# Two chunks of weights by plain products, and new durations for the order

## The chip, the cores and the metric

The kernel runs on one core of one Trainium2 chip. The metric is the time of one execution on the device in microseconds (us).

## The reference

Three parts follow each other. First comes linear attention with 4 batches, 8 heads, 576 tokens and a head size of 64; each head's output is normalised. Its 2304 tokens by 512 columns are x. Then x is multiplied by w_a and w_b (512 x 1536), the two results are multiplied element by element, and that by w_out (1536 x 512). Last comes a layer with a softmax in the middle.

```python
kv = einsum('bhsd,bhse->bhde', k, v)
o = einsum('bhsd,bhde->bhse', q, kv)
x = o / sqrt(mean(o * o, -1) + 1e-06) * g_norm     # to 2304 x 512
y = (x @ w_a) * (x @ w_b) @ w_out
h = y @ w_in                                       # 512 x 1024
s = h * softmax(h)
out = (s - mean(s)) / sqrt(var(s) + 1e-06) * g_ln @ w_out2
```

The weights arrive as 64-bit floats and are decoded on the chip.

## The kernel before

Each matrix product is made of float32 operands that are split in two: a high part (a copy rounded to the type that TensorE multiplies, `hi_of`) and a low part (what is left, `lo_of`). A product is then three matmuls, high by high, high by low and low by high (`three`, L668 to L671).

The work has three stages on TensorE.

1. Attention. Each of 20 tiles of at most 128 tokens goes through `att_1` (L557): a product with the matrix kv, a square and a copy on ScalarE, a sum on VectorE (L589), a power on GpSimd (L592) and a scaling on VectorE (L593). `att_2` (L598) transposes the tile on TensorE and writes it to x, scaled by g_norm (L620). Beside it the units of the products with w_a and w_b begin.
2. Those units (`Unit`, L682). x is cut into three thirds of 768 tokens, and each third into four quarters: A11, A12 are the upper and lower half of the 512 columns for the first 384 tokens; the other two belong to the second 384. The 1536 columns of w_a and w_b are cut into twelve chunks f of 128. For a chunk and a third, seven products of quarters (P1 to P7, `PROD`) take the place of eight. They need sums of quarters of x (S1 to S4, `x_blocks`, L630) and sums of quarters of the weights (T1 to T4, `w_sums`, L385). Each product has two halves of columns by three matmuls, so a unit has 42 matmuls of 384 columns. The results g go to DRAM.
3. The product with w_out (L1094): g and w_out come back from DRAM by `fetch` (L832), are split (L837, L838) and multiplied in six blocks of 384 tokens, y. Meanwhile w_in and w_out2 are decoded. Then the last layer runs (L1206, L1291, and L669 to L671 again).

Every chunk of weights is loaded in raw form by SyncE's queue (`load_one`, L262) and decoded by one ScalarE and five VectorE instructions and an addition (`decode`, L309 to L356).

The order of instructions on each engine is fixed when the kernel is built. The class `Order` (L46) keeps a clock for ScalarE ("A"), VectorE ("V") and GpSimd ("G"); each operation has a reckoned duration there. Where a tuple such as "GV" with two durations is given, the engine that would end sooner takes it, VectorE's duration counted twice (`PRICE`). Of operations that are due, the one of lowest rank goes first. TensorE's work is chosen by the main loop: `next_unit` (L846) has at most two units in work, of the first two chunks that are not through, and steps of attention go in between on a credit. DMAs of all kinds are issued by SyncE's queue, in the order in which the loop comes to them, and a DMA that waits holds those behind it.

In `x_blocks` the operations of third t have rank 1.2 + t and 1.1 + t; the tiles of attention have rank 1 + third. A tile of the last third waits in `back_ready` (L513) until its place in x4 is free.

## Time and profile before

| | before |
|---|---|
| median of 3 runs | 773.57 us (771.54 to 774.11) |
| profiled execution | 772.95 us, its span 771.0 us |
| TensorE busy | 699.9 us, 91% of the span |
| VectorE busy | 525.7 us, 68% |
| ScalarE busy | 313.0 us, 41% |
| GpSimd busy | 305.2 us, 40% |
| mean granted clock of TensorE | 0.96 |

The span goes from the first to the last instruction of the profiled execution; the time of that execution includes what lies around it. PE is TensorE, PEld its loads of weights, DVE VectorE, ACT ScalarE, POOL GpSimd, SPq the queue of SyncE. A clock of 1.00 is 2.4 GHz.

### The profile page before, as it was taken

Reading aid. Unit: us, or ns where it says so; the run is one execution under the profiler, and the core shown is the slowest. Engines: PE = TensorE matmul, PEld = TensorE weight load, DVE = VectorE, ACT = ScalarE, POOL = GpSimd, SP = SyncE. Lnnn points to the kernel's source line nnn. Section 1 sums busy time; section 2 is a strip of 40 time slices with the busy share of each in tenths; the row PEclk is TensorE's granted clock in tenths of the full one; section 3 lists DMA queues with packets and bytes.
Section 4 is the critical chain, followed back from the end, with each engine's and each line's share of the span. In section 5 each row is a group of like instructions: output and inputs, shape, how many; then the busy total and the mean of one; then the engine's idle time right before and its main releaser. Section 6 shows DMA issues by size and latency. Waiting matters only on the chain. (4 is left out here: it accounts for less than half of the span.)

```text
span 771.0 us, 10606 instructions
## 1 busy us (share of the span) xinstructions
PE 699.9 (91%) x3916; PEld 640.5 (83%) x3916; DVE 525.7 (68%) x792; ACT 313.0 (41%) x603; POOL 305.2 (40%) x272
## 2 busy tenths in 40 slices
PE   5768867889999998899989979998999999999998
PEld 4658756789998998889889979988987888888887
DVE  3768776687677777885366889786239494587661
ACT  3654734433333333322364444344144444344331
POOL 0655673344153334441372676423035353344110
PEclk9767978999999999999999989999999999999999
DMA  9725301044343433442286534675600000000001
GB/s 305 296 86 192 119 28 42 21 151 144 110 158 130 137 110 132 141 148 99 89 280 212 180 99 137 216 246 159 237 2 15 28 15 28 18 25 27 28 28 42
DMA packets 37652, 89.83 MB, mean 117 GB/s; under 512 B 4448, under 2 KB 14944, under 8 KB 37600
## 3 DMA queue, kind: packets, MB, share of 16 engines
q1 hardware_dynamic: 37600, 89.15, 33.6%
q8 instruction: 31, 0.51, 0.3%
q14 instruction: 21, 0.17, 0.1%
HBM read 62.92 MB, written 26.21 MB: 116 GB/s over the span
## 5 line engine op out<-in xcount | busy, mean ns | idle before, releaser
L1094 PE MATMUL ps<-regl,regh 128*128 128x384 f32 x384 | 74.4, 351 | 10.0 <-ACT y L1098 8.1
L1094 PEld LDWEIGHTS ps<-regl,regh 128*128 128x128 f32 x384 | 70.6, 199 | 12.5 <-ACT y L1098 9.7
L356 POOL TENSOR_TENSOR wf_w<-wf_w,u_w 128x512 f32<-128x512 f32 x20 | 27.2, 1360 | 80.8 <-DVE u_w L345 80.8
L669 PE MATMUL ps<-xh,wCh 128*128 128x384 f32 x144 | 51.2, 356 | 7.9 <-ACT xh L154 4.6
L592 POOL TENSOR_TENSOR r<-r,mhalf 128x8 f32<-128x8 f32 (+1 forms) x20 | 37.9, 1908 | 50.3 <-ACT r L591 41.5
L754 DVE TENSOR_TENSOR g<-ps,s 128x384 f32<-128x384 f32 x36 | 20.0, 556 | 54.1 <-PE ps L671 38.1
L669 PE MATMUL ps<-xh,wAh 128*128 128x384 f32 x144 | 50.6, 352 | 4.6 <-ACT xh L154 1.5
L838 DVE TENSOR_TENSOR regl<-regl 128x384 fp32r<-128x384 f32 x51 | 42.8, 856 | 17.0 <-ACT regl L837 16.7
L670 PE MATMUL ps<-xl,wBh 128*128 128x384 f32 x144 | 48.9, 340 | 5.9 <-DVE xl L640 5.9
L670 PE MATMUL ps<-xl,wCh 128*128 128x384 f32 x144 | 50.2, 349 | 4.3 <-DVE xl L640 4.3
L669 PE MATMUL ps<-xh,wBh 128*128 128x384 f32 x144 | 50.3, 349 | 3.4 <-ACT xh L154 1.3
L670 PE MATMUL ps<-xl,wAh 128*128 128x384 f32 x144 | 50.1, 348 | 1.2 <-POOL xl L640 1.2
L671 PE MATMUL ps<-xh,wCl 128*128 128x384 f32 x144 | 49.9, 346 | 0.5 <-POOL wCl L413 0.5
L671 PE MATMUL ps<-xh,wAl 128*128 128x384 f32 x144 | 50.2, 348 | 0.1
L671 PE MATMUL ps<-xh,wBl 128*128 128x384 f32 x144 | 48.6, 337 | 0.0
L736 ACT COPY ps<-ps 128x384 f32<-128x384 f32 x36 | 16.7, 464 | 76.4 <-PE ps L671 51.1
L837 ACT CAST regl<-regl 128x384 fp32r<-128x384 f32 (+1 forms) x56 | 28.9, 523 | 36.0 <-DMA regl<-gd 35.8
L1301 DVE TENSOR_TENSOR dl<-t,regl 128x1024 fp32r<-128x1024 f32 x18 | 21.8, 1218 | 30.6 <-ACT regl L1300 30.5
L1094 PE MATMUL ps<-regl,regl 128*128 128x384 f32 x228 | 40.5, 334 | 0.0
L1094 PEld LDWEIGHTS ps<-regl,regl 128*128 128x128 f32 x228 | 39.6, 188 | 0.0
L1206 PE MATMUL h<-bo,aop 128*128 128x512 f32 x150 | 38.2, 395 | 0.0
L669 PE MATMUL out<-regh,regl 128*128 128x512 f32 (+1 forms) x95 | 36.8, 387 | 1.1 <-DVE dl L1301 1.1
(172 smaller groups left out, 1966.7 us busy)
## 6 DMA issues: line engine op xcount, KB each, us to landing
raw_w<-in_w SPq DMA_DIRECT2D x36, 512.0 KB, 3.5
gd<-g SPq DMA_DIRECT2D x36, 384.0 KB, 2.3
regl<-gd SPq DMA_DIRECT2D x51, 192.0 KB, 3.1
kv<-in_kv SPq DMA_DIRECT2D x16, 512.0 KB, 6.6
out<-us SPq DMA_DIRECT2D x17, 256.0 KB, 2.0
raw_i<-in_w_in SPq DMA_DIRECT2D x8, 512.0 KB, 3.6
raw_o<-in_w_out SPq DMA_DIRECT2D x8, 512.0 KB, 4.1
so<-raw_o SPq DMA_DIRECT2D x8, 512.0 KB, 3.0
```

The costliest lines, as they stand in the source:

```text
L356: e.tensor_tensor(out=f, in0=f, in1=u, op=ALU.add)
L592: ("G", 1.75, lambda: nc.gpsimd.tensor_tensor(out=r[0:n], in0=r[0:n], in1=mhalf[0:n], op=ALU.pow)),
L669: nc.tensor.matmul(o, lhsT=ah, rhs=bh, start=first, stop=False, skip_group_check=skip)
L670: nc.tensor.matmul(o, lhsT=ah, rhs=bl, start=False, stop=False, skip_group_check=skip)
L671: nc.tensor.matmul(o, lhsT=al, rhs=bh, start=False, stop=last, skip_group_check=skip)
L736: od.chain([("A", 0.48, lambda: nc.scalar.copy(out=Y, in_=X)), od.mark("yc", f, t)], t=at)
L754: nc.vector.tensor_tensor(out=self.g[:, 1], in0=Y, in1=self.s5, op=ALU.add)
L837: ("A", costs[0], lambda: nc.scalar.copy(out=hi, in_=lo.bitcast(F32))),
L838: (costs[1], costs[2], lambda: e.tensor_tensor(out=lo, in0=lo.bitcast(F32), in1=hi.bitcast(F32), op=ALU.subtract)),
L1094: nc.tensor.matmul(o, lhsT=x[:, s], rhs=y, start=f == 0 and i == 0, stop=f == NF1 - 1 and i == 2)
L1206: nc.tensor.matmul(o, lhsT=x, rhs=y, start=first and k == m == 0, stop=k == 1 and m == 2, skip_group_check=not first)
L1301: ("V", 1.14, lambda: nc.vector.tensor_tensor(out=dl, in0=ps, in1=dh.bitcast(F32), op=ALU.subtract)),
```

## The change

For the chunks 0 and 1 (`NPL = 2`) a new class `Plain` makes plain products of a block of 384 tokens with w_a and w_b: 2 x 4 x 3 matmuls per block, two blocks in place of a unit. They need no sums of the weights or of x, but the quarter A21 itself, which is split to a place `a21` in the ring of weights of group C. Groups C and D of the weights are joined.

x is written by `att_2` directly as high and low part for the first 384 tokens of the first two thirds. The sums of x are made with ranks 2.6, 2.9 and 3.2, from the parts; there are seven additions or subtractions in place of four for each third, since a quarter that is only there as two parts is added in two steps. x4 lies in a new pool xt, and when the sums of the last third are split ("xfree", 2) a pool ph1b takes its place, which holds buffers that the seven-product units need: none of them starts before.

The reckoned durations of most operations are new: longer for VectorE's additions and subtractions (the low part of a fetched g 0.84 in place of 0.55), some shorter (decoding 3.23 in place of 3.45 in all). A buffer of raw weights is given back, and the next load issued, 1.0 us after its last reckoned use, and the stores of w_out and w_out2 0.8 us after. The last layer's weights lie in thirteen tiles of their own in place of ten and parts of x4.

```diff
...
+    xt = tc.alloc_tile_pool(name="xt", bufs=1, side="right")
+    ph1b = None
...
+            def give(t):
+                R_RAW.give(slot)
+                loads()
             if k[0] != "o":
-                R_RAW.give(slot)
-            loads()
+                od.chain([(None, 0, give)], t=t + 1.0)
...
-                od.chain([("GV", (1.32, 0.65), whole), od.mark("wf", k[1], k[2])], rank=rank - 0.01, t=t)
+                od.chain([("GV", (1.38, 0.95), whole), od.mark("wf", k[1], k[2])], rank=rank - 0.01, t=t)
...
         od.chain(
-            [("A", 0.6, a), ("V", 0.6, b1), ("V", 0.55, b2), ("V", 0.8, b3), ("V", 0.6, b4), ("V", 0.9, b5),
+            [("A", 0.67, a), ("V", 0.5, b1), ("V", 0.58, b2), ("V", 0.8, b3), ("V", 0.55, b4), ("V", 0.8, b5),
...
-    GROUPS = {"A": 512, "B": 512, "C": 512, "D": 256}
+    GROUPS = {"A": 512, "B": 512, "C": 768}
     WHERE = {"B11": ("A", 0), "B21": ("A", 256), "T2": ("B", 0), "B22": ("B", 256),
-             "T1": ("C", 0), "T3": ("C", 256), "T4": ("D", 0)}
-    LAST_OF = {"A": "P2", "C": "P7", "B": "P3", "D": "P4"}
+             "T1": ("C", 0), "T3": ("C", 256), "T4": ("C", 512)}
+    LAST_OF = {"A": "P2", "B": "P3", "C": "P4"}
+    NPL = 2
     wt = {}
...
+        if f < NPL:
+            split("B", 0, wf[:, 512:1024], 512, [("wf", f, 1)], "wf")
+            od.after([("wf", f, 0)], [used("ua")])
+            od.after([("wf", f, 1)], [used("ub")])
+            return
...
-        if third == 2:
-            for n in ((A11, A12, S2, S4), (S3, A22, S1))[half]:
-                when = max(when, od.at(("x", 1, n)))
+        if (third, half) == (2, 1):
+            when = max(when, od.at(("xfree", 0)))
...
+        direct = third < 2 and half == 0
+        if direct:
+            dh, dl = xh[third][:, 0:4, c0:c0 + n], xl[third][:, 0:4, c0:c0 + n]
+            od.chain([
+                ("A", 0.69, lambda: nc.scalar.activation(out=dh, in_=src, func=AF.Copy, scale=gn[:, 0:1])),
+                ("V", 0.75, lambda: nc.vector.scalar_tensor_tensor(
+                    out=dl, in0=src, scalar=gn[:, 0:1], in1=dh.bitcast(F32), op0=ALU.mult, op1=ALU.subtract)),
+                (None, 0, done),
+            ], rank=rank, t=od.now + 0.44 + 0.2)
+            return
...
+        def hi21(e):
+            a21[t] = tuple(o.rearrange("p (k c) -> p k c", k=2) for o in c_place(t))
+            copy_by(e, a21[t][0], low())
+        od.after([("x32", t, 1), ("wring", "C", t - 2)], [
+            ("AV", (0.83, 0.75), hi21),
+            ("VG", (1.15, 2.05), lambda e: e.tensor_tensor(
+                out=a21[t][1], in0=low(), in1=a21[t][0].bitcast(F32), op=ALU.subtract)),
+            od.mark("a21", t)], rank=r1)
+        split(A22, up, [("x32", t, 1)] + there, r1)
+        def s2_place(t_):
+            s2t[t] = xt.tile([P, 2, NB], F32, tag="s2", name=f"s2_{t}")
+        od.after([x[A22], ("a21", t)], [op(up, low, up, ALU.add), od.mark(*s[S1])], rank=r2)
+        od.after([s[S1], x[A11]] + [("xfree", t - 1)] * (t > 0), [
+            (None, 0, s2_place), op(temp, up, part(A11, False), ALU.subtract), op(temp, temp, part(A11, True), ALU.subtract),
+            od.mark(*s[S2])], rank=r2)
+        od.after([s[S1], x[A11]], [
+            op(low, part(A11, False), low, ALU.subtract), op(low, low, part(A11, True), ALU.add), od.mark(*s[S3])], rank=r2)
+        od.after([x[S2], x[A12]], [
+            op(temp, part(A12, False), temp, ALU.subtract), op(temp, temp, part(A12, True), ALU.add), od.mark(*s[S4])],
+            rank=r2)
+        split(S1, up, [s[S1], s[S2]][:1], r2)
+        split(S2, temp, [s[S2]], r2)
+        split(S3, low, [s[S3]], r2)
+        split(S4, temp, [s[S4]], r2)
+        od.after([x[n] for n in (S1, S2, S3, S4)], [od.mark("xfree", t)])
...
+            when = max(od.at(("x", t, a)), od.at(("w", f, WHERE[w][0], WHERE[w][1] if w == "T4" else 0)))
+            if ph1b is None or name == "P1" and banks_free() < 2 or name == "P5" and banks_free() < 1:
...
+    class Plain:
+        def __init__(self, f, j):
+            self.f, self.j, self.n = f, j, 0
+        def ready(self):
+            f, t, odd = self.f, self.j // 2, self.j % 2
+            m, kt = divmod(self.n, NP)
+            when = od.at(("w", f, "AB"[m], 0))
+            if m == 0:
+                k = ((("x", t, A11), ("x", t, A12)), (("a21", t), ("x", t, A22)))[odd][kt // 2]
+                when = max(when, od.at(k))
+            if self.n == 0 and banks_free() < 2:
+                return INF
+            return when
+        def run(self):
+            f, t, odd = self.f, self.j // 2, self.j % 2
+            m, kt = divmod(self.n, NP)
+            if self.n == 0:
+                started.add(f)
+                self.no = n_unit[0]
+                n_unit[0] += 1
+                self.bank = bank(False), bank(False)
+                part_used.difference_update(self.bank)
+            wh, wl = wt[f, "AB"[m]]
+            s = slice(kt * P, (kt + 1) * P)
+            if not odd:
+                bh, bl = xh[t][:, kt], xl[t][:, kt]
+            elif kt < 2:
+                bh, bl = (o[:, kt] for o in a21[t])
+            else:
+                bh, bl = (o(t, A22)[:, kt - 2] for o in (hi_of, lo_of))
+            three(bk(self.bank[m]), wh[:, s], wl[:, s], bh, bl, kt == 0, kt == NP - 1)
+            self.n += 1
+            if kt == NP - 1:
+                g = "AB"[m]
+                w_uses[f, g] = w_uses.get((f, g), 0) + 1
+                if w_uses[f, g] == NBLK:
+                    od.fire(("wring", g, f), od.now + G3)
+            if m == 0 and kt == NP - 1:
+                def a():
+                    self.g = ph1.tile([P, 2, NB], F32, tag="g", name=f"g{f}_{self.j}")
+                    nc.scalar.copy(out=self.g[:, 0], in_=bk(self.bank[0]))
+                od.fire(("pa", f, self.j), od.now + G3 + 0.1)
+                od.after([("pa", f, self.j), ("g", self.no - 2)], [("A", 0.48, a), bank_done(self.bank[0]), od.mark("pc", f, self.j)])
+            if self.n == 2 * NP:
+                def mult():
+                    nc.vector.tensor_tensor(out=self.g[:, 0], in0=bk(self.bank[1]), in1=self.g[:, 0], op=ALU.mult)
+                def store_g(when):
+                    if (f, t) not in gd:
+                        gd[f, t] = dr.tile([P, 2, NB], F32, tag=f"g{f}_{t}", name=f"gd{f}_{t}")
+                    nc.sync.dma_start(out=gd[f, t][:, odd], in_=self.g[:, 0])
+                    od.chain([od.mark("g", self.no), od.mark("gp", f, self.j)], t=od.load(4 * NB * P))
+                od.fire(("pb", f, self.j), od.now + G3 + 0.1)
+                od.after([("pc", f, self.j), ("pb", f, self.j)], [
+                    ("V", 0.56, mult), bank_done(self.bank[1]), (None, 0, store_g)])
+                over.add((f, self.j, 0))
+                if odd:
+                    od.after([("gp", f, self.j - 1), ("gp", f, self.j)], [od.mark("gd", f, t)])
+                    if all((x, self.j, 0) in over for x in range(NPL)):
+                        od.fire(("wring", "C", t), od.now + G3)
+                if all((f, j, 0) in over for j in (2 * t, 2 * t + 1)):
+                    unit_over(f, t)
...
-                fetch(r[:, 0:NB], r[:, NB:2 * NB], gd[f, j // 2][:, j % 2], 4 * NB * P, ("gy", j, f), (0.5, "V", 0.55), 0.5)
+                fetch(r[:, 0:NB], r[:, NB:2 * NB], gd[f, j // 2][:, j % 2], 4 * NB * P, ("gy", j, f), (0.52, "V", 0.84), 0.5)
...
+        if ph1b is None and ("xfree", 2) in od.done:
+            xt.release()
+            ph1b = tc.alloc_tile_pool(name="ph1b", bufs=2, side="right", reuse_waits="tile")
+            decode_more()
...
```

`c_place` takes a tile of 768 columns for each part from the ring; `behind` counts a plain block as half a unit.

## Rows read from the trace of the kernel before

**Rows 1.** Windows of all engines: stretch and length, busy us (instructions), clock, DMA.

```profile
core 0: us, PE busy (x) PEld busy (x) DVE busy (x) ACT busy (x) POOL busy (x), PEclk, DMA share, GB/s
17.00:128.40 111.40, 84.68 (x630) 74.53 (x628) 80.65 (x113) 61.41 (x140) 64.50 (x37) 0.82 0.38 137
128.40:141.50 13.10, 8.03 (x30) 7.05 (x31) 9.70 (x8) 6.90 (x11) 6.04 (x3) 0.74 0.04 13
160.00:394.20 234.20, 219.77 (x1222) 210.35 (x1221) 166.08 (x285) 81.57 (x162) 94.47 (x73) 1.00 0.39 137
394.20:564.00 169.80, 158.01 (x866) 155.19 (x865) 122.31 (x171) 68.67 (x136) 68.76 (x46) 0.96 0.56 183
540.00:560.00 20.00, 20.00 (x116) 19.97 (x116) 3.76 (x9) 1.83 (x4) 0.00 (x0) 1.00 0.68 230
564.00:771.00 207.00, 202.69 (x980) 168.27 (x978) 131.12 (x181) 83.52 (x134) 67.37 (x104) 1.00 0.06 24
```

**Rows 2.** Windows of line 669 alone: stretch and length, TensorE, weight loads, clock, DMA.

```profile
37.90:128.40 90.50, 23.47 (x56) 12.86 (x56) 0.82 0.28 98
128.40:160.00 31.60, 15.07 (x42) 8.55 (x42) 0.89 0.14 48
160.00:394.20 234.20, 139.01 (x407) 76.19 (x406) 1.00 0.39 137
```

**Rows 3.** Timeline of TensorE: start, length of the merged piece, operation, count.

```profile
408.72 4.32 PE L1094 MATMUL ps<-regl,regl 128*128 128x384 f32 x24
412.88 6.40 PE L1094 MATMUL ps<-regh,regl 128*128 128x384 f32 x36
```

**Rows 4.** Waits of TensorE, 17 to 160 us: in total, times, longest.

```profile
PE ps L670 <- DVE xl L640: 10.1, 5, 2.4
```

**Rows 5.** Timeline of ScalarE, VectorE and TensorE up to 132 us.

```profile
44.20 1.08 ACT L587 ACTIVATE sq<-ps 128x512 f32<-128x512 f32 x2
61.24 0.67 DVE L589 TENSOR_REDUCE r<-sq 128x8 f32<-128x512 f32 x1
74.63 1.03 PE L604 MATMUL ps<-ident,x 128*128 128x128 f32 x8
127.67 0.63 PE L604 MATMUL ps<-ident,x 128*128 128x128 f32 x4 [1.96 <-DVE x L593]
131.68 0.69 PE L670 MATMUL ps<-xl,wAh 128*128 128x384 f32 x1 [1.20 <-POOL xl L640]
```

**Rows 6.** Line 640 (ns: least/median/most), and line 754 (busy us, mean ns).

```profile
L640 DVE TENSOR_TENSOR xl<-x,xh x19: 940/953/2559, 34.3 to 140.5; 128x768 fp32r<-128x768 f32 x19
L754 DVE TENSOR_TENSOR g<-ps,s 128x384 f32<-128x384 f32 x36 | 20.0, 556 | 54.1 <-PE ps L671 38.1 <-issue 10.4 <-ACT u_w L326 3.5
```

**Rows 7.** Timeline of GpSimd and VectorE around 56 and 64 us.

```profile
55.48 2.48 POOL L645 TENSOR_TENSOR x<-x 128x768 f32<-128x768 f32 x1 [1.50 <-DVE x L645]
56.19 2.31 DVE L356 TENSOR_TENSOR wf_w<-wf_w,u_w 128x512 f32<-128x512 f32 x1
63.90 0.68 DVE L356 TENSOR_TENSOR wf_w<-wf_w,u_w 128x512 f32<-128x512 f32 x1
```

**Rows 8.** Waits of TensorE, 160 to 394.2 us.

```profile
PE ps L669 <- DVE g L754: 6.8, 6, 1.7
```

**Rows 9.** Timeline of SyncE's queue, ScalarE, TensorE, and TensorE's waits from 394.2.

```profile
446.54 0.33 SPq L262 DMA_DIRECT2D raw_o<-in_w_out  x1
450.81 0.51 ACT L837 CAST regh<-regh 128x384 fp32r<-128x384 f32 x1 [4.70 <-DMA regh<-gd]
453.60 8.82 PE L1094 MATMUL ps<-regl,regh 128*128 128x384 f32 x33 [3.96 <-ACT y L1098]
PE ps L1094 <- ACT y L1098: 9.9, 5, 4.0
```

**Rows 10.** Lines by form: line 838, with busy us and mean ns.

```profile
L838 DVE TENSOR_TENSOR regl<-regl 128x384 fp32r<-128x384 f32 x51 | 42.8, 856 | 17.0 <-ACT regl L837 16.7
L838 DVE TENSOR_TENSOR regh<-regh 128x384 fp32r<-128x384 f32 x21 | 16.4, 802 | 6.0 <-ACT regh L837 6.0
```

More of the change, by code (lines that the diff above doesn't have):

```diff
@@ L300, in decode_more @@
                     return
-            elif not R_F.ok():
+            elif not R_F.ok() or ph1b is None:
                 return
@@ L320, in decode @@
         else:
-            sf, f = R_F.take(), dec.tile([P, CH], F32, tag="f", name="f_" + nm, bufs=R_F.n)
+            sf = R_F.take()
+            f = (ph1b if k[0] == "w" else dec).tile([P, CH], F32, tag="f", name="f_" + nm, bufs=R_F.n)
         ub, fb = u.bitcast(U32), f.bitcast(U32)
@@ L606, in att_2 @@
         src = ps.rearrange("c (p t) -> c p t", t=P)[:, :, 0:n]
-        if third and (third, half) not in x4:
-            x4[third, half] = xs.tile([P, 4, NB], F32, tag=f"x4{half}", name=f"x4_{third}{half}")
-        dst = (x4[third, half] if third else x4[0][:, 4 * half:4 * half + 4])[:, :, c0:c0 + n]
+        rank = 1 + third
         def done(when):
@@ L615, in done @@
             if not x_left[third, half]:
-                od.fire(("x32", third, half), when)
+                if direct:
+                    od.fire(("x", third, A11), when)
+                    od.fire(("x", third, A12), when)
+                else:
+                    od.fire(("x32", third, half), when)
+        direct = third < 2 and half == 0
+        if direct:
+            dh, dl = xh[third][:, 0:4, c0:c0 + n], xl[third][:, 0:4, c0:c0 + n]
[6 more added lines that the diff above has]
+            return
+        if (third, half) not in x4:
+            x4[third, half] = xt.tile([P, 4, NB], F32, tag=f"x4{half}", name=f"x4_{third}{half}", bufs=1 + half)
+        dst = x4[third, half][:, :, c0:c0 + n]
         def scaled(e):
@@ L622, in scaled @@
                 e.tensor_scalar(out=dst, in0=src, scalar1=gn[:, 0:1], scalar2=None, op0=ALU.mult)
-        od.chain([
-            ("AV", (0.6, 0.65), scaled),
-            (None, 0, done),
-        ], rank=1 + third, t=od.now + 0.44 + 0.2)
+        od.chain([("AV", (0.69, 0.75), scaled), (None, 0, done)], rank=rank, t=od.now + 0.44 + 0.2)
+    a21, s2t = {}, {}
     def x_blocks(t):
-        rank = 1.2 + t
-        there = [("xok", t)] if t else []
-        t1, t2 = [("x32", t, 0)] + there, [("x32", t, 1)] + there
+        r1, r2 = 1.2 + t, 2.6 + 0.3 * t
+        there = [("xok", 2)] if t == 2 else []
+        x = {n: ("x", t, n) for n in range(7)}
@@ L654, in x_blocks, with op, part @@
-        add(S4, A12, S2, ALU.subtract, [s[S2]] + [x[A12]][:t])
-        for n in (S1, S2, S3, S4):
-            split(n, [s[n]])
+        def op(o, a, b, op):
+            return ("VG", (1.0, 2.05), lambda e: e.tensor_tensor(out=o(), in0=a(), in1=b(), op=op))
+        def part(n, lower):
+            return lambda: (lo_of if lower else hi_of)(t, n).bitcast(F32)
+        if t == 2:
+            for n in (A11, A12):
+                split(n, lambda n=n: x4[2, 0][:, 2 * n:2 * n + 2], [("x32", 2, 0)] + there, r1)
@@ L658, in attention_moe_moe_kernel @@
+        split(S1, up, [s[S1], s[S2]][:1], r2)
[3 more added lines that the diff above has]
+        od.after([x[n] for n in (S1, S2, S3, S4)], [od.mark("xfree", t)])
     for t in range(NTH):
         x_blocks(t)
-    def third_1(when):
-        xh[1] = xs.tile([P, 14, NB], F32R, tag="xh1", name="xh1")
-        od.fire(("xok", 1), when)
-    od.after([("x", 0, n) for n in range(7)], [(None, 0, third_1)])
     def three(o, ah, al, bh, bl, first, last, skip=False):
@@ L784, in post @@
                 unit_over(f, t)
-    units = {f: list(range(NTH)) for f in range(NF1)}
+    class Plain:
[26 more added lines that the diff above has]
+                bh, bl = (o[:, kt] for o in a21[t])
+            else:
+                bh, bl = (o(t, A22)[:, kt - 2] for o in (hi_of, lo_of))
[30 more added lines that the diff above has]
+                    unit_over(f, t)
@@ L787, in attention_moe_moe_kernel @@
+    units = {f: list(range(NBLK if f < NPL else NTH)) for f in range(NF1)}
     w_uses = {}
@@ L844, in attention_moe_moe_kernel, with behind @@
     ATT = 2.0
+    def behind(f):
+        return len(units[f]) * (1 if f < NPL else 2)
     def next_unit():
@@ L852, in next_unit @@
             for n, f in enumerate(two):
-                if n == 0 or len(units[f]) > len(units[two[0]]):
-                    u = Unit(f, units[f][0])
+                if n == 0 or behind(f) > behind(two[0]):
+                    u = (Plain if f < NPL else Unit)(f, units[f][0])
                     if u.ready() <= od.now:
@@ L914, in first_over @@
         nonlocal yp, wb, dec, bt, R_U, R_F, R_RAW, w_loads, dec_q
-        if yp is not None or dec_q or any(("w", f, g) not in od.done for f in range(NF1) for g in GROUPS) or any(
+        if yp is not None or dec_q or any(("wring", g, NF1 - 1) not in od.done for g in "AB") or any(
                 ("gd", f, t) not in od.done for f in range(NF1) for t in range(NTH)):
@@ L918, in first_over @@
         assert not any(k[0] == "w" for k in arrived)
+        ph1b.release()
         ph1.release()
```

143 lines of the change are left out of this document (68 added, 75 removed).

## The prediction

> **What bounds the kernel now.** The profiled execution took 772.95 us, of which the span is 771.0; the median of the three timed runs is 773.57, so the sum below is made against 772.95 and stands 0.62 us under the median.
>
> I first cut the span into stages, by where the lines of TensorE begin and end, and asked for the windows of all engines. The reader is to see that the limits differ [rows 1]. Up to 128.4 us attention runs; VectorE is busy 80.65 of 111.4 us, TensorE 84.68, and the clock is 0.82. From 160 to 394.2 the seven-product units fill TensorE (219.77 of 234.2). From 394.2 to 564 the product with w_out runs, and from 564 on TensorE is full (202.69 of 207).
>
> Busy time flatters a pipelined engine, so I counted work instead. 24 matmuls of 384 columns start at 408.72 and the next group at 412.88 [rows 3]: 4.16 us / 24 = 0.1733 us each at full clock. The line of the first of three matmuls has 56, 42 and 407 of them in the stretches up to 128.4, 160 and 394.2 [rows 2]; the two other lines have as many within one. So:
> - 37.9 to 128.4: 168 matmuls, four units of 42, 29.1 us of work in 90.5 us (attention shares it).
> - 128.4 to 160: 126, 21.8 us of 31.6; 9.8 lost.
> - 160 to 394.2: 1221, 211.6 us of 234.2; 22.6 lost, a factor of 1.107.
> - 394.2 to 564: six blocks of tokens by twelve chunks by four outputs by three, 864 matmuls, 149.7 us of 169.8; 20.1 lost.
>
> Then the waits. Early on TensorE waits 10.1 us for low parts of x [rows 4]. Late in the unit stage it waits 6.8 us for one VectorE addition [rows 8]. In the w_out stage it waits 9.9 us for copies of y [rows 9].
>
> **The change part by part.**
>
> *Plain products.* A unit of 42 matmuls becomes two blocks of 24, for two chunks and three thirds: 6 x (48 - 42) = 36 matmuls more, 36 x 0.1733 = 6.2 us of TensorE. The whole first stage then has 12 blocks x 24 = 288 and 30 units x 42 = 1260 matmuls, against 1512.
>
> *Where they stand.* The blocks need no sums of x. The new test in Unit.ready lets no seven-product unit start before the sums of the last third are split, since ph1b takes the place of xt. Queued behind that wait are all 1260 matmuls. So the stage falls in two: blocks beside attention, then units. Eight blocks (tokens of the first two thirds, 33.3 us) replace the four units (29.1 us) beside attention, where TensorE has idle time and half clock enough to hide 4.2 us more. Behind the end of attention, T, come four blocks and all units. Before, the first product of the last third ran freely from 131.68, 3.3 us behind 128.4 [rows 5]. I keep that: T + 3.3 + 96 x 0.1733 (16.6) + 1260 x 0.1733 x 1.107 (241.7) = T + 261.6. Before it was 394.2 - 128.4 = 265.8. The gain of 4.2 us comes from the four blocks: they have no copies between their products, so of the 9.8 us lost up to 160 only the 3.3 at the start stay, less some 2 us for the matmuls more. It holds if the sums are there at T + 19.9.
>
> *T itself.* A tile of the second third was squared at 44.20, and its reduction ran only at 61.24; its transposes came at 74.63 [rows 5]. In between VectorE had the sums and low parts of the first third, which the old ranks put ahead. The new ranks (2.6, 2.9, against 2 for the tiles of that third) put them behind it, but ahead of the last third's tiles (3). So the 17 us are not all won: the same work comes back before T. VectorE's work up to T, with a low part at 0.953 us, the addition that reads PSUM at 0.556 [rows 6] and scaling by columns (estimates from these rows):
> - gone: four low parts, 3.8; eight of sixteen multiplications and additions behind products, 4.4; five subtractions of weights (two of 512 columns at 0.64, three of 256 at 0.32), 2.2.
> - new: six low parts straight from PSUM, 6 x 0.556 x 512/384 = 4.4; two low parts for a21, 1.9; six more sums, 5.7.
> Net 1.6 us more. If VectorE keeps its share of 0.724 [rows 1], T is 1.6/0.724 = 2.2 later: 130.6. If no idle time were left, T is 17 + 80.65 + 1.6 = 99.3. I take 124.0, a quarter of the 17 us off 128.4, near the upper end, as the rows show one engine with as much work as before: 4.4 us gained.
>
> *Sums behind.* For the last third the stretch 128.4 to 141.5 held four sums and seven splits [rows 1]. Now there are seven sums and eight splits (a21 is split too): 13.1 x 15/11 = 17.9 us, against the 19.9 us that the blocks cover. The cover is 2 us thick; each microsecond past it is one of the span. The weights of chunk 2 need the room of chunk 0's, and a21's of the second third; they come free with the last blocks, and the B half of that block and the other chunk's block (36 matmuls, 6.2 us) cover one split.
>
> *Longer durations.* The order reckoned 0.55 us for a low part of g; the 51 and 21 of them took 0.856 and 0.802 [rows 10], 59.2 us against 39.6. VectorE was thus planned 19.6 us too fast in the w_out stage. What it does: the queue issues a load of raw weights at 446.54 when VectorE's last use is over; the fetch of g behind it lands so late that ScalarE waits 4.70 us for it, and the copies of y and TensorE (3.96 us idle) behind that [rows 9]. The 33 matmuls after it took 8.82 us and not 5.7 (0.267 us each: a part of them at the lower of the two clock levels): 7.1 us for one stall. The new figure of 0.84, and 1.0 us of distance before a load and 0.8 before a store, aim at this chain. The work of decoding has room behind it, since VectorE is busy 3.76 of the 20 us from 540 to 560 [rows 1]. The gain lies between all of the 20.1 and one more stall of this kind, -7.1. I take 4.0: more than half of one such stall, as nothing says which stalls go.
>
> *At nothing.* The last stage: TensorE was busy 202.69 of 207 [rows 1]; thirteen tiles in place of ten and three parts change no instruction. Twelve stores of half a g in place of six whole ones, and the pause before loads: SyncE's queue waits on engines, not on transfers; without that cover a chunk's decoding starts 1 us later, once per piece, and only where VectorE is idle.
>
> *GpSimd and VectorE.* An addition of 512 columns took 0.68 us on VectorE alone and 2.31 us where it began inside a GpSimd operation (55.48 to 57.96) [rows 7]. With the new costs 1.9 (0.95 times the price of 2) against 1.38 the order gives more of them to GpSimd. Twenty moved would free 13.6 us of VectorE or, each holding one of its operations for 1.63 us, take 32.6. I count nothing, midway; the wait of 6.8 us [rows 8] could go or double. The Trainium skill, SBUF — State Buffer, section "SBUF: two separate sides", says of the port pair of these two engines that it is an exclusive lock for a whole instruction, also against a VectorE operation with two SBUF inputs. The row agrees; by the rule the sum would be 6.8 us worse, which is the upper part of the first rival.
>
> **Sum.** 772.95 - 4.2 - 4.4 - 4.0 = 760.35; I say 760.
>
> **The rivals.**
>
> *Attention is no sooner.* The order changes but VectorE's work does not shrink: T = 130.6, and w_out loses what it lost. 772.95 - 4.2 + 2.2 = 771, up to 778 where GpSimd holds VectorE longer. For it: the work is 1.6 us more. Against it: 30.7 us of idle VectorE up to 128.4, and a tile standing 17 us.
>
> *The sums come too late (the other side).* The place is between the last block and the first unit; the point is 394.2 - 241.7 = 152.5 us. If attention of the last third drives the second third's seven sums and four splits behind T as well, 17.9 + 13.1 = 31 us follow T = 130.6, and the units start at 161.6: 403.3, 9.1 us later, 782. TensorE then idles some 11 us and the clock falls. For it: all 1260 matmuls hang on that one wait. Against it: the ranks put those sums ahead of the last tiles.
>
> *Both gains in full.* As forecast up to 394, and no stall left in w_out: 772.95 - 4.2 - 4.4 - 20.1 = 744. For it: the stalls are few and of one kind. Against it: other transfers wait in the same queue.
>
> **How the numbers follow.** Forecast 0.50 (its own range 750 to 768), attention no sooner 0.18, sums late 0.19, both in full 0.13. What can be told from no change is 0.3%, so 771.2 to 775.9. Faster: 0.50 + 0.13 + a quarter of 0.18 = 0.68. Same: half of 0.18 and a tenth of 0.19 = 0.11. Slower: 0.21. The range of 8 in 10 is 744 to 779.
>
> **What would show it.** After: 24 matmuls to each block from 30 us on; the last transposes near 124; the first seven-product unit before 152.5 and without idle time ahead of it; the first w_out product near 385; the w_out stage some 166 us long with fewer waits for y; 207 us behind it. The prediction is wrong if TensorE idles ahead of the first unit, if the stretch of units loses more than a factor of 1.11, or if w_out takes 170 us or more.

## The result, and the profile after

The changed kernel takes 748.36 us (median of 4 runs, 745.03 to 750.92) against 773.84 for the kernel before on the same chip: ratio 0.9672, 95% interval 0.9628 to 0.9716. The forecast was 760, faster. Its profiled execution took 748.11 us with a span of 746.3.

| | before | forecast | after |
|---|---|---|---|
| attention ends, T | 128.4 | 124.0 | 113.4 |
| from T to the first unit (blocks) | | 19.9 | 23.8 |
| units, to the first w_out product | | 241.7 | 247.2 |
| first w_out product at | 394.2 | 385.6 | 384.4 |
| w_out stage | 169.8 | 165.8 | 154.6 |
| last stage | 207.0 | 207.0 | 207.3 |
| profiled execution | 772.95 | 760.35 | 748.11 |

So 9.8 us come from the time up to the first w_out product, where 8.6 were forecast, and 15.2 from the w_out stage, where 4.0 were.

The windows of all engines, after, cut at the same events as [rows 1]:

```profile
core 0: us, PE busy (x) PEld busy (x) DVE busy (x) ACT busy (x) POOL busy (x), PEclk, DMA share, GB/s
17.00:113.40 96.40, 82.64 (x656) 71.11 (x654) 77.95 (x104) 55.88 (x128) 67.47 (x36) 0.93 0.44 156
113.40:137.20 23.80, 19.92 (x97) 19.52 (x98) 22.89 (x21) 9.99 (x17) 18.16 (x10) 0.78 0.11 42
137.20:384.40 247.20, 228.83 (x1261) 219.85 (x1261) 178.55 (x296) 83.92 (x168) 95.87 (x75) 0.99 0.38 133
384.40:539.00 154.60, 151.41 (x866) 149.42 (x865) 119.78 (x171) 68.41 (x135) 69.51 (x46) 1.00 0.60 200
539.00:746.30 207.30, 202.88 (x980) 168.32 (x978) 131.14 (x181) 83.93 (x135) 67.39 (x104) 1.00 0.06 24
```

In the first row VectorE is busy 77.95 of 96.4 us, 0.81 of the time against 0.724: its work fell by 2.7 us and its idle time from 30.7 to 18.5. Those 12.3 and 2.7 are the 15.0 that T came sooner. In the fourth row TensorE is busy 151.41 of 154.60.

The windows of the line of the first of three matmuls, now L723, as in [rows 2]:

```profile
0.00:113.40 113.40, 24.89 (x64) 12.47 (x64) 0.94 0.51 178
137.20:384.40 247.20, 144.56 (x420) 79.49 (x420) 0.99 0.38 133
```

64 x 3 = 192 matmuls before 113.4: eight blocks stand beside attention, as forecast. 420 x 3 = 1260 stand behind 137.2, worth 218.4 us at 0.1733; they took 247.2, a factor of 1.132 where 1.107 was forecast.

Timeline of TensorE at the end of attention, after (compare [rows 5]):

```profile
112.70 0.66 PE L616 MATMUL ps<-ident,x 128*128 128x128 f32 x4 [0.78 <-ACT x L648]
114.13 0.69 PE L723 MATMUL ps<-xh,wAh 128*128 128x384 f32 x1 [0.78 <-ACT x L648]
117.97 0.69 PE L724 MATMUL ps<-xl,wAh 128*128 128x384 f32 x1 [3.15 <-DVE xl L675]
```

The last transposes start at 112.70. The first product of the last third runs freely only from 117.97, 4.6 us behind T and not 3.3. Timelines of VectorE (first row) and GpSimd in that place:

```profile
115.36 5.05 DVE L675 TENSOR_TENSOR xl<-x,xh 128x768 fp32r<-128x768 f32 x2
115.02 2.08 POOL L695 TENSOR_TENSOR wCl<-x,wCh 128x768 fp32r<-128x768 f32 x1
117.06 2.54 POOL L675 TENSOR_TENSOR xl<-x,xh 128x768 fp32r<-128x768 f32 x1
```

Two low parts of x took 5.05 us, where one takes 0.953 [rows 6], while GpSimd was at work on operations that read two tiles: the same holding up as in [rows 7].

Timelines of ScalarE (two rows) and TensorE (last row) behind the first units:

```profile
147.94 0.62 ACT L156 CAST wCh<-u_w 128x512 fp32r<-128x512 f32 x1 [3.59 <-DVE u_w L408]
148.46 0.47 ACT L791 COPY ps<-ps 128x384 f32<-128x384 f32 x1
148.99 0.69 PE L723 MATMUL ps<-xh,wBh 128*128 128x384 f32 x1 [3.26 <-ACT ps L791]
```

ScalarE's copy for a unit (L791) stands in its queue behind a high part of chunk 3's weights, which waited 3.59 us for a subtraction of weights on VectorE. TensorE waits 3.26 us for that copy, and runs at the lower of its two clock levels behind it: up to 154.3 matmuls start 0.32 us apart, and not 0.1733. No sum of x is waited for here; the sums were in time, but the weights' work stood behind them on VectorE.

How much this place costs is seen when the stretch of units is divided 25 us behind its start (L723 alone):

```profile
137.20:162.20 25.00, 12.02 (x32) 6.64 (x32) 0.86 0.29 97
162.20:384.40 222.20, 132.54 (x389) 72.85 (x388) 1.00 0.39 137
```

The last of the 32 runs over the boundary and stands in both rows. So 93 matmuls of the three lines begin in the first 25 us, 16.1 us of work: 8.9 lost. The other 1167, 202.2 us, took 222.2, a factor of 1.099. There the forecast factor held; the loss beyond it is at the start.

In the w_out stage, after: TensorE's waits for copies of y and the queue's waits for VectorE's last use of raw weights (us in total, times, longest), then the low part of a fetched g in the view of lines by form (busy us, mean ns):

```profile
PE ps L1224 <- ACT y L1228: 2.6, 2, 1.4
SPq L258 <- DVE u_i L342: 6.1, 3, 3.3
```

```profile
L962 DVE TENSOR_TENSOR regl<-regl 128x384 fp32r<-128x384 f32 x51 | 42.1, 845 | 12.5 <-ACT regl L961 12.2
```

Before, the same wait of the queue was:

```profile
SPq L262 <- DVE u_i L345: 21.5, 8, 6.0
```

The low parts are about as long as in [rows 10], 845 ns against 856. What changed is the order: the queue waits 6.1 us behind raw weights in place of 21.5, and TensorE 2.6 us for y in place of 9.9 [rows 9].

### The profile page after: what moved, and what is told of

Same layout as the page of the kernel before. It is cut to its first block, busy times and chain, and to the rows that moved or that the text cites. A ratio compares the mean times of both kernels' runs of the same rounds, so it can differ in the third digit from the quotient of the medians.

```text
span 746.3 us, 10672 instructions
## 1 busy us (share of the span) xinstructions
PE 695.6 (93%) x3950; PEld 637.1 (85%) x3950; DVE 534.1 (72%) x782; ACT 305.9 (41%) x589; POOL 320.4 (43%) x277
## 4 chain that ended last, share of the span: by engine, by line
PE 47%; DMA 3%; DVE 3%; ACT 1%; POOL 1%; issue 0%; SPq 0%; ACTq 0%; DVEq 0%; POOLq 0%
PE ps L1224 18%; PE h L1336 10%; PE out L724 4%; PE out L725 4%; PE out L723 4%; PE t L1421 2%; DMA regh<-gd 1%; PE ps L723 1%; PE ps L725 1%; PE ps L724 1%; DMA gd<-g 1%; DMA regh<-swo 1%; DMA regl<-gd 0%; DVE st L1400 0%; ACT y L1228 0%
## 5 line engine op out<-in xcount | busy, mean ns | idle before, releaser
L1224 PE MATMUL ps<-regl,regh 128*128 128x384 f32 x384 | 69.1, 336 | 2.0 <-ACT y L1228 1.4
L723 PE MATMUL ps<-xh,wCh 128*128 128x384 f32 x180 | 62.2, 346 | 8.0 <-DVE g L809 4.1
L723 PE MATMUL ps<-xh,wBh 128*128 128x384 f32 x156 | 55.1, 353 | 7.3 <-ACT ps L791 6.1
L725 PE MATMUL ps<-xh,wCl 128*128 128x384 f32 x180 | 61.0, 339 | 0.8 <-POOL wCl L421 0.8
L724 PE MATMUL ps<-xl,wCh 128*128 128x384 f32 x180 | 61.0, 339 | 0.0
L723 PE MATMUL ps<-xh,wAh 128*128 128x384 f32 x156 | 55.1, 353 | 5.2 <-DVE g L809 1.7
L1336 PE MATMUL h<-bo,aop 128*128 128x512 f32 x195 | 46.6, 395 | 0.0
L723 PEld LDWEIGHTS ps<-xh,wCh 128*128 128x128 f32 x180 | 34.4, 191 | 11.7 <-DVE g L809 5.8
L791 ACT COPY ps<-ps 128x384 f32<-128x384 f32 x30 | 13.9, 463 | 74.2 <-PE ps L725 53.0
L1431 DVE TENSOR_TENSOR dl<-t,regl 128x1024 fp32r<-128x1024 f32 x18 | 21.8, 1218 | 30.6 <-ACT regl L1430 30.5
L1336 PEld LDWEIGHTS h<-bo,aop 128*128 128x128 f32 x195 | 36.2, 188 | 7.8 <-ACT bt L1354 0.3
L723 PEld LDWEIGHTS ps<-xh,wBh 128*128 128x128 f32 x156 | 29.8, 191 | 11.7 <-ACT ps L791 9.6
```

The source lines that it names most:

```text
L723: nc.tensor.matmul(o, lhsT=ah, rhs=bh, start=first, stop=False, skip_group_check=skip)
L724: nc.tensor.matmul(o, lhsT=ah, rhs=bl, start=False, stop=False, skip_group_check=skip)
L725: nc.tensor.matmul(o, lhsT=al, rhs=bh, start=False, stop=last, skip_group_check=skip)
L791: od.chain([("A", 0.48, lambda: nc.scalar.copy(out=Y, in_=X)), od.mark("yc", f, t)], t=at)
L1224: nc.tensor.matmul(o, lhsT=x[:, s], rhs=y, start=f == 0 and i == 0, stop=f == NF1 - 1 and i == 2)
L1336: nc.tensor.matmul(o, lhsT=x, rhs=y, start=first and k == m == 0, stop=k == 1 and m == 2, skip_group_check=not first)
```

## The experiments

Stages are read from the one profiled execution of each run; where that stands more than 3 us off the run's median, it is said. The executions of one kernel lie up to 10.8 us apart (e8, 769.54 to 780.30), so differences of 3 us or so between single stages are not told apart.

| run | median us | ratio to before (95%) | T | T to first w_out product | w_out stage |
|---|---|---|---|---|---|
| after | 748.36 | 0.9672 (0.9628 to 0.9716) | 113.4 | 271.0 | 154.6 |
| e1 | 755.04 | 0.9767 (0.9735 to 0.9799) | 112.9 | 271.5 | 162.5 |
| e2 | 753.95 | 0.9750 (0.9700 to 0.9800) | 125.4 | 265.1 | 154.8 |
| e3 | 760.28 | 0.9849 (0.9792 to 0.9906) | 113.2 | 270.6 | 169.4 |
| e4 | 748.05 | 0.9683 (0.9653 to 0.9712) | | | |
| e5 | 738.31 | 0.9537 (0.9508 to 0.9565) | 116.7 | 260.3 | 154.3 |
| e6 | 760.94 | 0.9829 (0.9805 to 0.9854) | 116.8 | 280.5 | 154.2 |
| e7 | 746.59 | 0.9645 (0.9619 to 0.9671) | 110.8 | 267.4 | 157.6 |
| e8 | 773.13 | 0.9998 (0.9969 to 1.0027) | 113.0 | 290.0 | 157.8 |
| e9 | 761.63 | 0.9851 (0.9825 to 0.9877) | 113.0 | 268.3 | 171.3 |
| e10 | 759.90 | 0.9838 (0.9804 to 0.9872) | 123.1 | 270.4 | 157.1 |
| e11 | 756.92 | 0.9802 (0.9760 to 0.9843) | 116.0 | 278.9 | 157.4 |
| e12 | 757.78 | 0.9789 (0.9742 to 0.9835) | 116.3 | 278.5 | 154.6 |

### Are there two gains, and which edit brings which?

**e1_old_durations.** The changed kernel, reckoned with the durations of before and without pauses:

```diff
...
-            [("A", 0.67, a), ("V", 0.5, b1), ("V", 0.58, b2), ("V", 0.8, b3), ("V", 0.55, b4), ("V", 0.8, b5),
+            [("A", 0.6, a), ("V", 0.6, b1), ("V", 0.55, b2), ("V", 0.8, b3), ("V", 0.6, b4), ("V", 0.9, b5),
...
-                fetch(r[:, 0:NB], r[:, NB:2 * NB], gd[f, j // 2][:, j % 2], 4 * NB * P, ("gy", j, f), (0.52, "V", 0.84), 0.5)
+                fetch(r[:, 0:NB], r[:, NB:2 * NB], gd[f, j // 2][:, j % 2], 4 * NB * P, ("gy", j, f), (0.5, "V", 0.55), 0.5)
...
```

> The changed kernel with the durations and pauses of before in the order; the plain blocks, the direct write of x and the ranks stay. Theory (two gains apart: the blocks and ranks shorten the time to the first w_out product, the durations the w_out stage): last transposes near 115 us, first w_out product near 386, the w_out stage about 170 long as before; time about 764. Rival (the durations make both): last transposes near 125, first w_out product 392 or later, w_out 170; time 770 or more. Second rival (the w_out stage is shorter through the other places of buffers, not the durations): w_out about 155, time about 749.

Measured: 755.04; T 112.9, first w_out product at 384.4, w_out 162.5. The first gain is there in full without the new durations. The w_out stage lies between the two theories: half of its gain is there as well.

**e2_new_durations.** The kernel before, reckoned with the new durations and with the pauses:

```diff
...
-                fetch(r[:, 0:NB], r[:, NB:2 * NB], gd[f, j // 2][:, j % 2], 4 * NB * P, ("gy", j, f), (0.5, "V", 0.55), 0.5)
+                fetch(r[:, 0:NB], r[:, NB:2 * NB], gd[f, j // 2][:, j % 2], 4 * NB * P, ("gy", j, f), (0.52, "V", 0.84), 0.5)
...
```

> The kernel before with the changed kernel's durations and pauses, for all operations that both have; no plain blocks, ranks of x as before. Theory (two gains apart): first w_out product near 394 us, w_out stage near 155, time about 759. Rival (the durations make both): first w_out product near 385, w_out 155, time about 749. Second rival (neither comes from the durations alone): time within 3 us of 773.

Measured: 753.95; first w_out product at 390.5. The w_out stage, as a window of all engines, and its wait for y:

```profile
390.50:545.30 154.80, 151.53 (x867) 149.61 (x866) 117.94 (x170) 68.44 (x135) 68.65 (x46) 1.00 0.62 200
```

```profile
PE ps L1097 <- ACT y L1101: 2.7, 5, 1.0
```

154.80 us long with 2.7 us of waits: the durations and pauses bring the whole gain of that stage to a kernel without plain blocks. The 390.5 lies between the two theories, 3.7 us sooner than before.

**e3_fetch_cost.** The changed kernel with only the durations of a fetched g set back:

```diff
-("gy", j, f), (0.52, "V", 0.84), 0.5)
+("gy", j, f), (0.5, "V", 0.55), 0.5)
```

> The changed kernel with only the durations of a fetched g set back (0.5 and 0.55 in place of 0.52 and 0.84). Theory (VectorE planned 19.6 us too fast is what stalled the w_out stage): w_out stage 165 to 170, time 759 to 764. Rival (the pauses before loads and stores do it): w_out about 155 to 157, time 748 to 751. Up to the first w_out product all is as in the changed kernel, near 384.

Measured: 760.28; w_out 169.4. TensorE's waits for y and the queue's behind raw weights in that stage:

```profile
PE ps L1224 <- ACT y L1228: 11.5, 4, 6.2
SPq L258 <- DVE u_i L342: 22.6, 8, 3.8
```

11.5 us of waits for y, and 22.6 us of the queue behind raw weights: the figures of before are back, by one line of the plan. All else new in this order, the pauses among it, does not help without it. But e1, with this line old as well, lost only 12.8 (162.5 - 149.7), though its queue waited 19.3 us behind raw weights, so how many stalls come is not fixed by the line alone.

**e4_no_pause.** The pauses taken out:

```diff
-                od.chain([(None, 0, give)], t=t + 1.0)
+                od.chain([(None, 0, give)], t=t)
...
-            (None, 0, lambda t: od.chain([(None, 0, out_to)], t=t + 0.8)),
+            (None, 0, out_to),
```

> The changed kernel without the pauses (1.0 us before a load of raw weights, 0.8 us before the stores of decoded w_out and w_out2). Theory (the fetch's duration does it): w_out stage 155 to 158, time 748 to 751; SyncE's queue waits longer for VectorE's last use than with the pauses. Rival (the pauses do it): w_out 165 to 170, time 759 to 764. The stage of units may lose up to 5 us, since loads there wait the same way.

Measured: 748.05, no change. The profiled execution was the longest of five (755.57), so its stages are not in the table; even in it w_out took 157.2 us, and the queue waited 8.8 us for VectorE's last use, a little longer as the theory has it. The pauses are worth nothing that can be told.

### What ends attention sooner?

**e5_sums_first.** The sums of x ahead of the next third's attention again:

```diff
-        r1, r2 = 1.2 + t, 2.6 + 0.3 * t
+        r1, r2 = 1.2 + t, 1.1 + t
```

> The changed kernel with the sums of x at rank 1.1 + t, ahead of the next third's attention, as in the kernel before; all else as changed. Theory (attention ends 15 us sooner because the sums no longer stand ahead of its tiles): last transposes 120 us or later, first w_out product 388 to 394, time 752 to 758. Rival (it ends sooner because products of the first blocks need no sums, and TensorE's order no longer waits): last transposes 112 to 116, time 746 to 751.

Measured: 738.31, faster than the changed kernel, outside both expectations. The last transposes, and the windows behind:

```profile
115.76 1.09 PE L616 MATMUL ps<-ident,x 128*128 128x128 f32 x4 [1.28 <-DVE x L605]
```

```profile
core 0: us, PE busy (x) PEld busy (x) DVE busy (x) ACT busy (x) POOL busy (x), PEclk, DMA share, GB/s
116.70:140.00 23.30, 19.17 (x88) 17.16 (x87) 21.77 (x18) 8.85 (x14) 15.82 (x8) 0.82 0.07 26
140.00:377.00 237.00, 229.11 (x1269) 218.83 (x1270) 179.06 (x297) 86.01 (x173) 95.74 (x76) 1.00 0.41 141
```

T is 3.3 us later, so the rival is near the truth: beside the rest of the change the ranks matter little for T. But the stretch behind T is 10.7 us shorter. The 420 matmuls of the first of three lines that belong to units:

```profile
141.75:377.00 235.25, 143.90 (x420) 78.71 (x420) 1.00 0.41 142
```

235.25 us, a factor of 1.077 of 218.4 against 1.132. Where the changed kernel waited 3.26 us for ScalarE's copy, no wait of TensorE between 141 and 175 is over 0.7 us. The first 25 us of units, as above for the changed kernel:

```profile
141.75:166.75 25.00, 14.87 (x44) 8.18 (x44) 1.00 0.42 135
```

130 matmuls of the three lines begin there (the last of the 44 again runs over the boundary), 22.5 us of work: 2.5 us lost where the changed kernel lost 8.9. That is 6.4 of the 12.0 us by which the stretch of units is shorter; the other 5.6 lie further on. With the sums of the first two thirds done early, VectorE could have less to do when the units start; that this makes the difference is argued from the two traces and not shown, since no further run was made on it.

**e9_ranks_alone.** The kernel before with the new ranks for the sums and their splits:

```diff
...
-                op=op)), od.mark("xs", t, o)], rank=rank - 0.1)
+                op=op)), od.mark("xs", t, o)], rank=2.6 + 0.3 * t)
...
-            split(n, [s[n]])
+            split(n, [s[n]], 2.6 + 0.3 * t)
```

> The kernel before with the new ranks alone for the sums of x and their splits (2.6, 2.9, 3.2); no plain blocks, old durations. If ranks are what ends attention sooner: last transposes 118 us or earlier. If it is that the first blocks need no sums, so that TensorE's order, with attention's steps in it, does not wait for them: here the units still need the sums, which now come later, so last transposes 122 us or later, TensorE's waits for xl and xh at 18 us or more in all, time 770 to 785.

Measured: 761.63; the last transposes:

```profile
112.39 0.60 PE L604 MATMUL ps<-ident,x 128*128 128x128 f32 x4
```

T is 113.0, with no plain block and old durations, and the first w_out product comes at 381.3, no later than in the changed kernel (384.4). So the ranks alone suffice, and e5 shows that the rest of the change nearly suffices without them. They are two ways to the same 12 to 15 us; they do not add.

**e12_no_direct.** The direct write taken out:

```diff
-        direct = third < 2 and half == 0
+        direct = False
...
-        if t == 2:
+        if True:
             for n in (A11, A12):
-                split(n, lambda n=n: x4[2, 0][:, 2 * n:2 * n + 2], [("x32", 2, 0)] + there, r1)
+                split(n, lambda n=n: x4[t, 0][:, 2 * n:2 * n + 2], [("x32", t, 0)] + there, r1)
```

> The changed kernel without the direct write: the first 384 tokens of the first two thirds are written whole and then split, as those of the last third; six low parts from PSUM go, four low parts of 768 columns and four high parts come. If the direct write is what ends attention sooner: last transposes 119 to 124 us, time 752 to 758. If it is the blocks that need no sums: last transposes 111 to 116, time 745 to 751.

Measured: 757.78, the time of the first theory; but T is 116.3, 2.9 us later, at the edge of the second. So the direct write is not what ends attention sooner. The stretch behind T is 7.5 us longer, and of TensorE's waits there the largest is

```profile
PE ps L723 <- DVE g L809: 11.9, 8, 3.2
```

VectorE's addition for a unit, 11.9 us against 5.8 with the direct write. That is the price that the trace shows; why it falls there was not followed further.

### Are the blocks the cover?

**e8_npl1.** Plain blocks for the first chunk alone (the ring of group C is counted on accordingly):

```diff
-    NPL = 2
+    NPL = 1
```

> The changed kernel with plain blocks for the first chunk alone: six blocks of 24 and 33 units, 18 matmuls (3.1 us) fewer, and half the work for TensorE beside attention and the sums. Theory (the blocks are the cover): four blocks (16.6 us) beside attention, two (8.3 us) behind it against 18 to 24 us of sums, so TensorE idles 10 to 16 us ahead of the first unit; first w_out product 398 to 408, time 763 to 773. Rival (attention ends sooner with fewer products beside it and the sums follow): last transposes 108 or earlier, time 746 to 755.

Measured: 773.13 (the profiled execution 769.54), no faster than before; T 113.0, first w_out product at 403.0. The size is as the theory has it, the place is another:

```profile
98.14 0.69 PE L616 MATMUL ps<-ident,x 64*128 64x64 f32 x4 [13.99 <-DVE x L605]
```

```profile
PE ps L616 <- DVE x L605: 24.4, 10, 14.0
```

TensorE stood idle 14.0 us in one piece ahead of the transposes at 98.14, and waited 24.4 for scaled tiles in all, since it had run out of blocks beside attention: between 84 and 113 it has no product of a block. The units follow at 130.1 and take 272.9 us, 1.136 times their 240.2. The second chunk's blocks are worth 24.8 us by the medians (21.4 by the two profiled executions). Without them three units more, 21.8 us of work, stand behind T; with them, four of six blocks fill TensorE ahead of it. The kernel of e9 fills it with units. TensorE from 17 to 113, first e9, then e8:

```profile
17.00:113.00 96.00, 76.33 (x623) 67.61 (x621) 79.11 (x108) 60.82 (x136) 70.59 (x39) 0.88 0.43 154
17.00:113.00 96.00, 62.87 (x553) 53.32 (x553) 77.98 (x104) 54.48 (x125) 73.61 (x39) 0.86 0.43 153
```

T is 113.0 in both and 113.4 in the changed kernel, at granted clocks of 0.88, 0.86 and 0.93: neither TensorE's work beside attention nor its clock accounts for T here.

### VectorE or GpSimd?

**e6_price_one.** VectorE's price halved:

```diff
-PRICE = 2.0
+PRICE = 1.0
```

> The changed kernel with the price of VectorE at 1.0 in place of 2.0, so the order gives about 31 of GpSimd's 265 operations more to VectorE. Theory of the shared port (an operation of GpSimd holds up one of VectorE): VectorE's operations of two inputs get shorter on the mean, the stretch from the last transposes to the first w_out product falls from 271 to 262 to 268 us, time 740 to 746. Rival (VectorE is what the units wait for): that stretch grows to 273 or more, time 750 to 760. No effect: 747 to 750.

Measured: 760.94; T is 116.8, and the stretch behind it 280.5 us, as the rival has it. Windows at nearly the same times as in the changed kernel (here the units end only at 397.3):

```profile
core 0: us, PE busy (x) PEld busy (x) DVE busy (x) ACT busy (x) POOL busy (x), PEclk, DMA share, GB/s
17.00:113.00 96.00, 78.61 (x642) 69.42 (x641) 73.60 (x114) 49.00 (x113) 48.04 (x27) 0.93 0.41 149
137.00:384.00 247.00, 227.25 (x1214) 215.92 (x1213) 180.06 (x318) 76.39 (x153) 54.77 (x45) 0.95 0.34 116
```

In the second window GpSimd is busy 54.77 us and not 95.87, and VectorE runs 318 instructions in 180.06 us, where it ran 296 in 178.55. In the first, where attention runs, GpSimd is busy 48.04 us and not 67.47. The scaling of an attention tile, the same sixteen instructions in both kernels, in the view of lines by form from 17 to 397 us, the changed kernel first and then e6:

```profile
L605 DVE TENSOR_TENSOR x<-x,r 128x512 f32<-128x512 f32 x16 | 18.3, 1149 | 2.2 <-POOL r L604 2.2
```

```profile
L605 DVE TENSOR_TENSOR x<-x,r 128x512 f32<-128x512 f32 x16 | 10.9, 684 | 1.8 <-POOL r L604 1.7
```

1149 ns a piece became 684: VectorE was indeed held up less. The time is worse by 12.6 us all the same. TensorE now waits for high parts of weights, one made by VectorE and two by ScalarE, for which the changed kernel shows no wait:

```profile
PE ps L723 <- DVE wAh L156: 4.7, 1, 4.7
PE ps L723 <- ACT wAh L156: 4.5, 2, 2.3
```

The theory of the port is right on the length of an operation and wrong on the time.

**e7_x_on_v.** Low parts and sums of x on VectorE alone:

```diff
...
-                ("VG", (1.15, 2.05), lambda e: e.tensor_tensor(
+                ("V", 1.15, lambda: nc.vector.tensor_tensor(
...
```

> The changed kernel with all low parts and sums of x after attention's direct ones on VectorE alone (ten or so leave GpSimd). Theory of the shared port: the two low parts of the last third that took 5.05 us together behind the last transposes take some 2 us, blocks start 2 to 3 us sooner, time 744 to 747. Rival (VectorE is full up to there, 78 of 96 us, and gets later): last transposes 116 or later, time 751 to 756.

Measured: 746.59, with an interval (0.9619 to 0.9671) that overlaps the changed kernel's: not told apart. The low parts behind the last transposes did get shorter:

```profile
113.50 2.68 DVE L675 TENSOR_TENSOR xl<-x,xh 128x768 fp32r<-128x768 f32 x3
```

Three took 2.68 us, where two took 5.05 beside GpSimd.

**e10_sums_price3.** Sums first, and a higher price:

```diff
-        r1, r2 = 1.2 + t, 2.6 + 0.3 * t
+        r1, r2 = 1.2 + t, 1.1 + t
...
-PRICE = 2.0
+PRICE = 3.0
```

> Sums first (as in the earlier run with rank 1.1 + t) and a price of VectorE of 3.0 in place of 2.0: some 20 operations more to GpSimd. If VectorE is what the units wait for: the stretch from the last transposes to the first w_out product falls from 260 to 255 to 258 us, time 733 to 737. If GpSimd's operations hold VectorE up by as much: 262 to 268, time 740 to 746.

Measured: 759.90; T 123.1, the stretch behind it 270.4. Worse than sums first by 21.6 us and outside both expectations, with the price moved the other way than in e6.

**e11_sums_x_on_v.** Sums first, and the edit of e7:

```diff
-        r1, r2 = 1.2 + t, 2.6 + 0.3 * t
+        r1, r2 = 1.2 + t, 1.1 + t
...
-            return ("VG", (1.0, 2.05), lambda e: e.tensor_tensor(out=o(), in0=a(), in1=b(), op=op))
+            return ("V", 1.0, lambda: nc.vector.tensor_tensor(out=o(), in0=a(), in1=b(), op=op))
...
```

> Sums first, and all low parts and sums of x after the direct ones on VectorE alone. If the gain of some 2 us seen without sums first came from the low parts behind attention: time 734 to 737. If sums first already took that up, or VectorE is the fuller for it: 739 to 745.

Measured: 756.92 (the profiled execution 761.43); T 116.0, the stretch behind it 278.9. 18.6 us worse than sums first alone and outside both expectations, where the same edit without sums first changed nothing that can be told.

These four move 17 to 34 of GpSimd's some 400 operations to or from VectorE. Three of them cost 12.6 to 21.6 us, whichever way the operations went, and the fourth changed nothing. No theory of one engine explains that; what it is beyond the accident of one order or another stays open. So does, with it, how much of the 10 us of e5 is the sums' place and how much the luck of its order.

## Why the prediction was right in sign, and short by 12 us

The direction, the size of the first stage in sum, the place of the blocks and the untouched last stage held. 748.36 lies outside the forecast's own range (750 to 768) and inside that of 8 in 10 (744 to 779). The rival *Both gains in full*, 744 at a chance of 0.13, came nearest: most stalls of w_out did go. And one of the three signs of being wrong came true: the stretch of units lost a factor of 1.132, over 1.11. Three terms were mis-sized.

- *Longer durations*, 4.0 forecast, 15.2 measured. The mechanism was right (a fetch behind a load that waits for VectorE, ScalarE behind the fetch, TensorE behind the copy of y), and so was the cause, 0.55 reckoned for 0.85: e3 shows it in the changed kernel by setting that line back, and e2, with all new durations, brings the gain to the kernel before. I took little more than half of one stall because nothing said which stalls go. The planned lag itself, 19.6 us over the stage, was the better guide: the loss was 20.1 before, 4.9 after.
- *T*, 4.4 forecast, 15.0 measured. I held T near its upper end since VectorE's work stayed the same. It did, nearly (2.7 us less, where I reckoned 1.6 more), but 12.3 of its 30.7 idle us went. I saw one standstill, 17 us in [rows 5], and let three quarters of it come back. In the timeline of TensorE the transposes stand still twice: from 48.41 to 74.63 before, and, in a place that I had left out, from 89.72 to 111.59:

```profile
48.41 0.68 PE L604 MATMUL ps<-ident,x 64*128 64x64 f32 x4
89.72 0.60 PE L604 MATMUL ps<-ident,x 128*128 128x128 f32 x4
111.59 1.01 PE L604 MATMUL ps<-ident,x 128*128 128x128 f32 x8
```

There the old order keeps the last third's transposes until splits of the second third are done (the test in back_ready). Its first tile was scaled at 93.52, and the last low part of the second third began at 108.19 (timeline of VectorE, before):

```profile
93.52 0.69 DVE L593 TENSOR_TENSOR x<-x,r 128x512 f32<-128x512 f32 x1
108.19 0.95 DVE L640 TENSOR_TENSOR xl<-x,xh 128x768 fp32r<-128x768 f32 x1
```

After:

```profile
46.84 0.46 PE L616 MATMUL ps<-ident,x 64*128 64x64 f32 x4
58.73 0.60 PE L616 MATMUL ps<-ident,x 128*128 128x128 f32 x4
80.83 0.63 PE L616 MATMUL ps<-ident,x 128*128 128x128 f32 x4 [0.45 <-DVE x L605]
82.71 0.60 PE L616 MATMUL ps<-ident,x 128*128 128x128 f32 x4
87.67 0.46 PE L616 MATMUL ps<-ident,x 64*128 64x64 f32 x4 [0.17 <-DVE g L891]
99.51 0.63 PE L616 MATMUL ps<-ident,x 128*128 128x128 f32 x4 [1.45 <-DVE x L605]
```

The first stand, between the first and the second third, has gone from 26.2 to 11.9 us. The second, between the second third (last at 80.83) and the last (first at 82.71), is gone: the new test holds back only the second half of the last third. In its place the transposes stand for 11.8 us inside the last third, from 87.67 to 99.51, while VectorE and GpSimd work on the second third's sums:

```profile
92.00 2.60 DVE L680 TENSOR_TENSOR s<-s,xl 128x768 f32<-128x768 f32 x1
91.29 2.49 POOL L680 TENSOR_TENSOR x<-x,xl 128x768 f32<-128x768 f32 x1 [0.90 <-DVE x L680]
```

That is the work that I let come back before T, and there it is. In e9, which keeps the old test, the stands are at the old places, 17.2 and 20.5 us; in e5 they are at the new ones, 20.0 and 13.6. Either way T comes out within 4 us of the same. A stand is thus no measure of what T gains, neither the one that I took nor the two.

- *Behind T*, a gain of 4.2 forecast, a loss of 5.2 measured. The blocks took 23.8 in place of 19.9 (a start held up by GpSimd's operations, and a granted clock of 0.78), the units 247.2 in place of 241.7. I took the factor 1.107 from a stretch in which the sums were long done, and behind the first 25 us it held (1.099). The gain was to come from the 9.8 us lost between 128.4 and 160, which I let go with the blocks; 8.9 us are lost again in the first 25 us of units, where TensorE waited behind chunk 3's weights. That is a part of the slower rival's mechanism, with another queue: the sums pushed back seem to cost, though not as a wait for sums. In e5, where they come early, this loss is 2.5 us and the kernel 10 us faster; how much of that is the sums' place stays open, as said above.

The errors on T and behind it nearly cancelled, so that 385.6 forecast and 384.4 measured agree for no good reason.

On GpSimd I counted nothing. The rows after agree with what the Trainium skill, SBUF — State Buffer, section "SBUF: two separate sides", says of the exclusive lock (5.05 us for two low parts, 1149 ns against 684 in e6). As a price on the whole it was not found: e6, which takes 41 us of GpSimd's work out of that window of the units, is slower.

The best kernel of the study is e5, 738.31 us, ratio to before 0.9537 (0.9508 to 0.9565), which beats both. Not run: the kernel before with new ranks and new durations together; by e9's 381.3 and e2's 154.8, with 207 and 2 around, it would be an estimated 745 without any plain block. So no run shows that the plain blocks are worth anything beside the new ranks and durations; what is shown is that within the changed kernel the second chunk's are (e8). More than two plain chunks were not tried.

## What to carry to other kernels

Compare the durations that a hand-made plan reckons with, line by line, with the trace, and start with the line that is most often run: here one line that was 0.3 us short on 72 operations cost 14.8 us of the w_out stage and 11.9 of the time (e3), through a queue that holds what stands behind a waiting load. When work is put behind other work to end a stage sooner, look at what has to start right after that stage on the same engine. And where a factor of loss is carried from one stretch to another, ask whether the engines beside it will be as free there as they were.

## What the runs showed that was not expected

Two edits that each end attention 12 to 15 us sooner (e9: 113.0, e5: 116.7) bring no more together (113.4). And in this kernel's plan moving some two dozen operations lengthens the stretch from T to the first w_out product from 260.3 to 278.9 us (e5, e11), more than most of the edits are worth.
